# A Fourier mix with four mirrored tokens folded into each partition, and an order of work read from a table

## The chip, the cores and the metric

One core of a Trainium2 chip runs the whole program. The metric is device time in microseconds (us), from the first instruction to the last of one execution. TensorE (PE) does matrix products, VectorE (DVE), ScalarE (ACT) and GpSimd (POOL) work on elements, SyncE (SP) and POOL start DMAs. Each engine carries out its own instructions strictly in the order in which the program holds them, and waits on semaphores for the others.

## The reference

Three layers follow one another on 4 batches of 768 tokens, with 8 heads of 40 features (320 in all): a recurrence, a layer that mixes by Fourier transforms and a dense network, and a layer that mixes tokens by a network and then channels.

```python
for t in range(S):                                   # attention
    y[:, :, t] = einsum('bhd,bhde->bhe', rt, state)
    Sa = einsum('bhde,bhe->bhd', state, at)
    state = state * wt - outer(Sa, bt) + outer(vt, kt)

X = fft(fft(x, axis=1), axis=2)                      # moe: tokens (768), then features (320)
u = x + real(X)
un = (u - mean(u)) / sqrt(var(u) + 1e-6)
x = u + maximum(un @ w_ch1, 0) @ w_ch2               # 320 -> 1280 -> 320

h = maximum(xT @ w_tok1, 0) @ w_tok2                 # moe2: 768 -> 256 -> 768 over tokens
u = x + hT
out = u + maximum(u @ w_ch1, 0) @ w_ch2              # 320 -> 1536 -> 320
```

The input is real and only the real part of the transform is used: real(X)[t, f] = sum over tokens and features of x times cos(token angle + feature angle). So the sums of one token frequency t at feature frequency f are those of 768-t at 320-f.

## The kernel before

**Accuracy.** Products run in a reduced float32 form (fp32r) on two parts of each number: a high part that is rounded to 12 bits and the rest. One product is then three matmuls: high by high, high by low, low by high. Some matmuls are plain float32.

**Attention.** 768 tokens are cut in 12 chunks of 64. Per chunk there are decay scans on DVE, an inverse of a small matrix, and products on PE: `sc` (line 509), `y` (lines 527 and 531), `x`, `z`, `s`. The output y of chunks 0 to 8 goes through DRAM (`xd`) and is loaded into the token tiles `X`, [128 tokens, 6 tiles, 4 batches, 320]; that of 9 and 10 goes straight to X by DMA; that of the last is written by DVE (line 537).

**First transform, `fft(b)`, batch by batch.** Twice (even and odd frequencies): tiles k and k+3 are added or subtracted into F (line 845), features folded into `ef` (846 to 848), split into Xh on ACT (851, 854) and Xl on DVE (852, 855), and multiplied by the token table T1: pairs of a matmul by Xh with 384 or 388 columns (line 866) and one by Xl with half of them (line 867). There are 24 such pairs for a batch. ACT and DVE take the sums out of PSUM into five tiles A (873, 875, 877), and ACT copies each mirrored to columns 385 to 768 (881).

**Second transform, `fft2(b)`.** Six groups of 128 tokens, each 8 matmuls `mix` with 320 columns (line 896); DVE adds each to X (898) and takes the statistics of the norm (899, 900).

**Network.** `turn(b, half)` norms and turns 3 tiles of 128 tokens (`trp`, line 957, and `th`, `tl`); `ch` then runs per 128 hidden units a group `hps` of 8 matmuls (986), the positive part hh on ACT (988), the rest hl on DVE (989), and a group `acc` of 9 matmuls (976). There are 80 such groups on W1, W2 (the first dense network) and 96 on v1, v2.

**Weights.** They lie in DRAM as 64-bit floats and are taken apart on the chip: a `job` (line 807 on) loads 64-bit raw data (`mdraw`), has four DVE instructions (819, 820, 822, 823), one on ACT (821) and two on POOL (824, 825), and writes both parts to DRAM (m11h, m11l for W2), from where POOL's queue loads them (line 795). Two sets of buffers carry the jobs in turn.

**Order.** The program is written as operations with a cost, a due time, reads and writes. `Plan.emit` (line 100 on) puts them in order before the kernel is built: each engine takes the ready operation with the earliest due time, by modelled costs and a table of shifts. Where the model sees PE idle it puts fillers, `warm` matmuls (line 52) whose result nobody reads; each shows as two instructions in the trace.

The order on an engine that matters most is that behind the last y: what remains of fft(0), fft2(0), turn, fft(1), and the jobs for W2 all stand on DVE together.

Of the kernel before, what the change touches and what calls it, by code (L numbers as in the profile page):

```python
# [26 lines left out]
YB='y'

def layouts(r,k,v,w,a,b):
    def heads(x,fill=0.0):  # L30
# [23 lines left out]
DMAC={('dec2',0.61):(0.91, 0.31),('dec2',1.25):(1.56, 0.75),('inv',0.42):(0.05, 2.19),('inv',1.69):(1.13, 1.55),('kg',0.85):(1.63, 1.11),('kg',0.9):(1.03, 1.07),('load',0.05):(0.05, 1.78),('load',1.4):(1.4, 1.63),('load',2.82):(2.85, 2.04),('load2',1.46):(1.67, 1.54),('load3',1.3):(1.4, 1.7),('load3',1.92):(2.53, 1.39),('loada',0.71):(0.96, 1.53),('merge',0.45):(0.53, 1.47),('merge',0.9):(0.97, 1.13),('out_tile',1.2):(1.93, 0.12),('out_tile',2.4):(2.86, 0.57),('outp',0.46):(0.4, 1.24),('wdec',0.6):(0.62, 1.6),('wdec',1.2):(1.08, 1.88)}  # L54
LDMA=.81

class Op:
# [4 lines left out]
LATE_SAME={'DVE':.118,'ACT':.12,'POOL':.12}

class Plan:

    def __init__(s,banks):
        s.ops=[]; s.w={}; s.r={}; s.banks=banks; s.stage=None; s.filler=None
    def op(s,eng,cost,fn,R=(),W=(),due=None,alloc=None,free=(),data=0.0,rel=0.0,after=(),cols=0.0,pools=None,port=None,lag=.4,nd=8,cls=0,bulk=0):
        if eng=='SP' and s.stage: data,lag=DMAC.get((s.stage[0],round(data,2)),(data,lag))
        o=Op(); o.cols=cols; o.cls=cls; o.bulk=bulk; o.stage=s.stage; o.pools=pools; o.lag=lag; o.nd=nd; o.port=(eng=='POOL' and not data) if port is None else port; o.rel=rel; o.eng,o.cost,o.fn,o.due,o.data=eng,cost+EXTRA.get(eng,0.0),fn,due,data  # L70
        o.alloc=[] if alloc is None else alloc if isinstance(alloc,list) else [alloc]
        o.free=tuple(free); o.idx=len(s.ops); o.succ=[]
# [10 lines left out]
        for d in o.deps: s.ops[d].succ.append(o.idx)  # L83
        s.ops.append(o); return o
    def lat(s,a,b):
        if a.eng==b.eng: return .2 if a.eng=='SP' else LATE_SAME.get(a.eng,0.0)
        return LATE.get(a.eng,.2)
    def dur(s,o): return o.cost+ (1.8+o.data if o.eng=='SP' or o.data else 0)
    def grant(s,b):
        while s.seen<b:  # L90
            s.seen+=1; x=s.seen
            s.low[x]=sum(s.cols.get(y,0.0) for y in range(x-NBK,x))<HT
        return 1.0-.5*sum(s.low.get(y,True) for y in range(b-NBK+1,b+1))/NBK
    def pe(s,t,o):

        w=o.cost; c=o.cols/w; dt=TICK/NBK
        if o.cls!=s.cls: t+=SW; s.cls=o.cls
        while w>1e-9:
            k=int(t/dt); f=s.grant(k)
            d=min(w/f,(k+1)*dt-t+1e-6); w-=d*f; t+=d  # L100
            s.cols[k]=s.cols.get(k,0.0)+c*d*f
            s.hist.append((t-d,t,c*f))
        return t
    def emit(s,end,slack):
        s.cols={}; s.hist=[]; s.cls=0; s.low={}; s.seen=0
        ops=s.ops
        lst=[0.0]*len(ops)
        for o in reversed(ops):
            t=end if o.due is None else o.due
            for j in o.succ: t=min(t,lst[j]-(s.lat(o,ops[j])+s.dur(o))*slack)  # L110
            lst[o.idx]=t
        for o in ops:
            if o.stage: lst[o.idx]+=OFF.get(o.stage[0],0.0)+OFF.get(o.stage,0.0)
        engines={e:0.0 for e in ('PE','ACT','DVE','POOL','SP','NONE')}
        cand={e:[] for e in engines}
        def put(o):
            o.ready=max([o.rel]+[ops[d].fin+s.lat(ops[d],o) for d in o.deps]); cand[o.eng].append(o)
        for o in ops:
            o.nwait=len(o.deps); o.fin=None
        for o in ops:  # L120
            if o.nwait==0: put(o)
        dma=0.0; held=[None,0.0]; ring=[]; pushed=0
        def port(o): return held[1] if o.port and held[0]!=o.eng else 0.0
        free={b:[0.0]*n for b,n in s.banks.items()}; s.bank={}
        left={}
        for o in ops:
            for h in o.free: left[h]=left.get(h,0)+1
        n=0; pools=()
        def fill(t,end):

            w=sum(r*(min(b,end)-max(a,end-TICK)) for a,b,r in s.hist[-80:] if b>end-TICK)
            if w>=FILL[1]: return
            b=next(((b,j) for b in pools for j,x in enumerate(free[b]) if x<=t),None)
            m=0; top=-int(-(FILL[1]-w)//512); o=Op(); o.eng='PE'; o.idx=-1; o.cls=0; o.deps=[]; o.cost=FILL[0]; o.cols=512.0; a=t+.1
            while b and m<top and a+FILL[0]<=end: a=s.pe(a,o); m+=1
            if m==0: return
            o.cost=a-t; o.fin=a; o.nd=m; free[b[0]][b[1]]=a+.3; s.trace.append((t,o)); s.nfill+=m
            if not DRY: s.filler(*b,m)
# [1020 lines left out]
```

## Time and profile before

| | |
|---|---|
| median of 3 runs | 999.69 us |
| lowest, highest | 997.78, 1010.21 us |
| span of the profiled execution | 998.0 us |
| mean granted TensorE clock, share of full | 0.974 |
| PE busy | 940.2 us (94%) |
| DVE busy | 632.2 us (63%) |
| ACT busy | 439.2 us (44%) |
| POOL busy | 271.0 us (27%) |
| fft and fft2, PE: lines 866, 867, 896 | 29.9, 24.8, 31.0 us |

The span is that of one execution under the profiler; it is 1.7 us below the median of the timed runs. Busy times of neighbours on PE overlap, since one matmul begins while the one ahead is still draining, so the length of a row is more than what it adds; what it adds is read from one start to the next. A digit of the page's slices is the busy share of about 25 us in tenths.

### The profile page before, as it was taken

How to read it: one execution, taken by the hardware profiler on the slowest of the kernel's cores; microseconds unless marked ns; L12 is line 12 of the kernel's file. 1: busy time of each engine (PE TensorE's matmuls, PEld its weight loads, DVE VectorE, ACT ScalarE, POOL GpSimd, SP SyncE). 2: the span in 40 equal slices, each digit the busy share in tenths (PEclk: the TensorE clock that was granted, in tenths of full speed). 3: DMA queues.
4: the chain of work that ended last, by engine and by line, in shares of the span. 5: the costliest groups of instructions: out<-in, count | busy, mean ns of one | idle time of the engine just before them, and what ended most of it. 6: DMA issues, size and time to landing. Idle time of an engine off the chain costs nothing.

```text
span 998.0 us, 23467 instructions
## 1 busy us (share of the span) xinstructions
PE 940.2 (94%) x9571; PEld 893.7 (90%) x9571; DVE 632.2 (63%) x1401; ACT 439.2 (44%) x910; POOL 271.0 (27%) x372
## 2 busy tenths in 40 slices
PE   7548999999999998999999999999999999999998
PEld 6447788788788887899999999999999999999998
DVE  8799497878849348899799984324342632423332
ACT  5266879789697674333342322223221312112121
POOL 8123544344653524243343435000000000000000
PEclk9788999999899899899999999999999999999999
DMA  9986878999787788354454456800000201101110
GB/s 212 200 188 139 185 181 171 184 200 213 162 190 180 180 237 290 117 180 138 146 186 131 162 159 217 310 1 1 1 20 24 92 21 48 68 20 49 44 44 20
DMA packets 144750, 132.53 MB, mean 133 GB/s; under 512 B 101059, under 2 KB 121539, under 8 KB 144515
## 3 DMA queue, kind: packets, MB, share of 16 engines
q1 hardware_dynamic: 139843, 107.36, 42.7%
q0 software_dynamic: 4800, 23.67, 6.9%
q8 instruction: 75, 1.23, 0.5%
q14 instruction: 32, 0.26, 0.1%
HBM read 88.94 MB, written 37.29 MB: 126 GB/s over the span
## 4 chain that ended last, share of the span: by engine, by line
PE 52%; DVE 6%; DMA 1%; issue 1%; ACT 0%; SPq 0%; DVEq 0%; ACTq 0%
PE hps L986 22%; PE acc L976 21%; PE t2ps L1063 2%; PE tps L1050 2%; PE mix L896 2%; DMA mdraw<-in_moe_w_tok_dram 1%; PE psA L866 1%; PE trp L957 1%; DVE mda L820 1%; PE warm L52 1%; PE psA L867 0%; DVE F L845 0%; DVE hl L989 0%; DVE Xl L852 0%; DVE A L875 0%
## 5 line engine op out<-in xcount | busy, mean ns | idle before, releaser
L989 DVE SCALAR_TENSOR_TENSOR hl<-hps,hh 128x384 fp32r<-128x384 f32 x176 | 97.7, 556 | 225.3 <-ACT hh L988 224.5
L988 ACT ACTIVATE hh<-hps 128x384 fp32r<-128x384 f32 x176 | 86.2, 490 | 321.2 <-PE hps L986 320.9
L986 PE MATMUL hps<-th,v 128*128 128x384 f32 x576 | 142.4, 337 | 0.0
L976 PE MATMUL acc<-v,hh 128*128 128x320 f32 x576 | 128.0, 309 | 0.0
L986 PE MATMUL hps<-th,W 128*128 128x384 f32 x480 | 120.3, 339 | 1.2 <-DVE hl L989 0.8
L976 PE MATMUL acc<-W,hh 128*128 128x320 f32 x480 | 107.4, 310 | 0.5 <-DVE X L999 0.5
L986 PEld LDWEIGHTS hps<-th,v 128*128 128x128 f32 x576 | 103.7, 188 | 0.0
L976 PEld LDWEIGHTS acc<-v,hh 128*128 128x128 f32 x576 | 98.1, 188 | 0.0
L976 PE MATMUL acc<-v,hl 128*128 128x320 f32 x288 | 89.0, 309 | 0.0
L986 PEld LDWEIGHTS hps<-th,W 128*128 128x128 f32 x480 | 86.8, 187 | 2.3 <-DVE hl L989 1.5
L976 PEld LDWEIGHTS acc<-W,hh 128*128 128x128 f32 x480 | 81.2, 188 | 0.8 <-ACT hh L988 0.8
L824 POOL TENSOR_TENSOR mda<-mda,mdh 128x320 f32<-128x320 f32 (+2 forms) x44 | 44.7, 1016 | 122.3 <-ACT mdh L821 62.8
L329 POOL TENSOR_SCALAR_AFFINE_SELECT RT<-RT 64x384 f32<-64x384 f32 x72 | 53.5, 767 | 82.1 <-ACT RT L238 78.4
L976 PE MATMUL acc<-W,hl 128*128 128x320 f32 x240 | 74.0, 308 | 0.0
L319 PE MATMUL kg<-am,bt 120*128 120x192 f32 x242 | 51.3, 351 | 21.3 <-ACT am L238 18.1
L986 PE MATMUL hps<-tl,v 128*128 128x384 f32 x192 | 64.6, 337 | 0.0
L319 PEld LDWEIGHTS kg<-am,bt 120*128 120x128 f32 x242 | 40.3, 198 | 26.3 <-ACT am L238 18.9
L519 POOL TENSOR_SCALAR_AFFINE_SELECT sc<-sc 64x384 f32<-64x384 f32 (+1 forms) x72 | 41.5, 577 | 73.1 <-ACT sc L238 61.4
L509 PE MATMUL sc<-rm,VZd 120*128 120x192 f32 x264 | 57.7, 354 | 2.2 <-DMA VZd<-in_vR_dram 1.5
L52 PE MATMUL warm<-ident 128*128 128x128 f32 x346 | 52.0, 297 | 4.5 <-DVE A L877 2.5
L976 PEld LDWEIGHTS acc<-v,hl 128*128 128x128 f32 x288 | 54.1, 188 | 0.0
L986 PE MATMUL hps<-tl,W 128*128 128x384 f32 x160 | 53.9, 337 | 0.0
(176 smaller groups left out, 2025.0 us busy)
## 6 DMA issues: line engine op xcount, KB each, us to landing
bt<-in_bkR_dram SPq DMA_DIRECT2D x12, 660.0 KB
mdraw<-in_moe_w_ch_dram SPq DMA_DIRECT2D x22, 320.0 KB
wS<-in_wR_dram SPq DMA_DIRECT2D x12, 335.2 KB
a<-in_aR_dram SPq DMA_DIRECT2D x12, 335.2 KB
RT<-a SPq DMA_DIRECT2D x36, 111.7 KB
LT<-in_vT_dram SPq DMA_DIRECT2D x12, 330.0 KB
VZt<-in_vT_dram SPq DMA_DIRECT2D x12, 330.0 KB
VZd<-in_vR_dram SPq DMA_DIRECT2D x12, 330.0 KB
```

Of the source, the lines that this page charges most:

```text
L52: for x in range(m): nc.tensor.matmul(t[:,128*(x%4):128*(x%4)+128],lhsT=ident,rhs=ident,start=True,stop=True)
L319: nc.tensor.matmul(ps[:,192*x:192*x+192],lhsT=bt[:,g+x].rearrange("p v t -> p (v t)"),rhs=am[:,:,g+x],start=True,stop=True)
L329: nc.gpsimd.affine_select(out=kv,in_=kv,pattern=[[0,3*m],[1,L]],compare_op=ALU.is_gt,fill=0.0,base=0,channel_multiplier=-1)
L509: for x,g in enumerate(gs): nc.tensor.matmul(ps[:,192*x:192*x+192],lhsT=VZd[:,g].rearrange("p v t -> p (v t)"),rhs=s.rm[:,:,g],start=True, ...
L519: nc.gpsimd.affine_select(out=o,in_=o,pattern=[[0,3*m],[1,L]],compare_op=ALU.is_gt,fill=0.0,base=0,channel_multiplier=-1)
L824: P.op('POOL',.07+d*.00237,lambda: nc.gpsimd.tensor_tensor(out=g("da").bitcast(F32),in0=g("da").bitcast(F32),in1=g("dh").bitcast(F32),op=A ...
L896: nc.tensor.matmul(s.pst(h)[:,:320],lhsT=aa[:K,sl],rhs=T2[:K,tb],start=n==0,stop=n==7)
L976: nc.tensor.matmul(s.pst(acc[x]),lhsT=a[:,sl],rhs=t[w2][w][:,m],start=(m==0 and n==0),stop=(m==MT-1 and n==2))
L986: for n,(l,r) in enumerate(ops): nc.tensor.matmul(ps,lhsT=l,rhs=r,start=n==0,stop=n==7)
L988: s.act(384,lambda: nc.scalar.activation(out=t["hh"][z],in_=s.pst(h),func=AF.Relu),[kp],[('hh',z)],free=[h[0]])
L989: s.dve(.47,lambda: nc.vector.scalar_tensor_tensor(out=t["hl"][z],in0=s.pst(h),scalar=0.0,in1=t["hh"][z].bitcast(F32),op0=ALU.max,op1=ALU. ...
L1050: nc.tensor.matmul(s.pst(h),lhsT=t["k1"][x][:,k,ms],rhs=t[a][:,k],start=k==0 and n==0,stop=k==5 and n==2)
```

## The change

The tokens are laid out anew, so that partition p of tiles 0, 1 (and of 3, 4) holds tokens that are mirrors of one another: tile 0 holds p+1, tile 1 383-p, tile 3 767-p, tile 4 385+p; tiles 2 and 5 hold the 128 that remain twice over in halves. The attention writes y in that layout, for six chunks in reversed order of tokens, with a few more and shorter DMAs through `xd`; the host permutes the rows of w_tok1, w_tok2 and of the output to match.

The first transform adds and subtracts tile k and k+3 (FP, FM), folds features (ef), and then adds and subtracts tiles 0 and 1 (sd): a sum runs over 128 partitions and two parts where it ran over three. The table has 416 columns a frequency kind. Per batch there are 8 pairs (a matmul of 416 columns by Xh, one of 208 by Xl), one more matmul of 208 columns (Ds), and 9 plain float32 matmuls `psA` with 64 columns of weights and 208 moving columns (T1f), whose results go to the lower or the upper half of the partitions. Only 385 token frequencies are formed.

```diff
-                                nc.tensor.matmul(ps[:,:2*cn],lhsT=t["Xh"][:,k,o:o+128],rhs=T(k,tb,par,2*cn),start=n==1 and k0==0,stop=False)
-                                nc.tensor.matmul(ps[:,:cn],lhsT=t["Xl"][:,k,o:o+128],rhs=T(k,tb,par,cn),start=False,stop=n==w and k1==3)
...
+            for n,op in (("FP",ALU.add),("FM",ALU.subtract)):
+                s.dve(.06+.336*w,lambda n=n,op=op,K=K,k0=k0,k1=k1: V.tensor_tensor(out=t[n][:,K,:320],in0=x()[:,K],in1=x()[:,3+k0:3+k1],op=op),xk+['mid0',(n,'pad')],kk(n),port=True)
...
+                for z,op in enumerate((ALU.add,ALU.subtract)):
+                    s.dve(.44,lambda z=z,op=op: V.tensor_tensor(out=t["sd"][:,z],in0=t["ef"][:,0],in1=t["ef"][:,1],op=op),e2(0,1)+['mid'],[('sd',z)],port=True)
+            def split(z,src,rd):
+                s.act(353,lambda: nc.scalar.activation(out=t["Xh"][:,z],in_=src(),func=AF.Copy),rd+['mid'],[('Xh',z)])
+                s.dve(.44,lambda: V.tensor_tensor(out=t["Xl"][:,z],in0=src(),in1=t["Xh"][:,z].bitcast(F32),op=ALU.subtract),rd+[('Xh',z)],[('Xl',z)],port=True)
...
+            z=2 if part else (par if kind==0 else 1-par); tk=2*kind+par; o=pst(h)[r]
+            out=[(t["Xh"][:,z,cs],T(part,tk,TC),o[:,:TC]),(t["Xl"][:,z,cs],T(part,tk,HC),o[:,:HC])]
+            if part and kind==0 and par==1: out.append((t["Ds"][:,cs],at.T1[:,8*TC:8*TC+HC],o[:,:HC]))
...
+                            nc.tensor.matmul(pst(h)[64*par:64*par+64,:HC],lhsT=sd(part,par if kind==0 else 1-par)[:,TS[kind]],rhs=TF(part,2*kind+par),start=part==1 and kind==0,stop=part==0 and kind==1,skip_group_check=True)
+                    if part: nc.tensor.matmul(pst(h)[64:128,:HC],lhsT=t["dd"][:,TS[0]],rhs=at.T1f[:,4*TC:4*TC+HC],start=False,stop=False,skip_group_check=True)
```

The second transform has four groups of 8 matmuls with 322 columns. Each sum is added to X forward for one token and with its features reversed for the mirror token, so a batch has 7 adds on DVE (three forward of 128 rows, four mirrored of 128, 128, 96 and 32 rows) instead of 6. ACT's mirrored copies of A go.

```diff
-        for i in range(6):
-            xk=s.at.xb(i,b) if s.first[b] else []
+        for i,(r,cs) in enumerate(((slice(0,128),slice(0,128)),(slice(0,128),slice(256,384)),(slice(0,128),slice(128,256)),(slice(0,128),slice(288,416)))):
...
+            def mi(q,rows):
+                s.dve(.4,lambda h=h: V.tensor_tensor(out=x(q,rows),in0=s.pst(h)[rows,320:0:-1],in1=x(q,rows),op=ALU.add),[kp]+xk(q)+['pend'],[('x',q,b)],free=[h[0]])
```

The jobs of the weights have four sets of buffers instead of two (three for those of W2):

```diff
-        nc=s.nc; V=nc.vector; P=s.P; d=dh.shape[-1]; q=dl.shape[0]; j=0 if nm=="w2" and n<WE else n%2; due=rel+40
+        nc=s.nc; V=nc.vector; P=s.P; d=dh.shape[-1]; q=dl.shape[0]; j=n%3 if nm=="w2" else n%4; due=rel+40
```

The planner goes. A long string, `ORDER`, names every operation in the order in which it is emitted, its PSUM buffer, and the fillers (`+count,bank,buffer`):

```diff
-    def emit(s,end,slack):
+    def emit(s):
...
+        for x in ORDER.split():
+            if x[0]=='+':
+                m,b,j=x[1:].split(','); assert (b,int(j)) not in held
+                s.filler(b,int(j),int(m)); continue
+            x,_,js=x.partition(':'); o=ops[int(x,36)]
+            assert o.idx not in done and all(d in done for d in o.deps)
...
+            o.fn(); done.add(o.idx)
```

**PE, the end of the attention.** Before, from the last filler ahead of the last y on; `psA` with Xh and Xl are sums of fft(0), whose first 8 pairs already stand further up, between steps of the last chunk.

```order
L52 MATMUL warm<-ident 128x128 x2
L527 MATMUL y<-Sbd_151,r_139 64x120
L531 MATMUL y<-kbt_149,sc_154 64x40 x3
L52 MATMUL warm<-ident 128x128
L866 MATMUL psA_5211<-T_4831,Xh 128x388
L867 MATMUL psA_5211<-T_4831,Xl 128x194
L866 MATMUL psA_5211<-T_4831,Xh 128x388
L867 MATMUL psA_5211<-T_4831,Xl 128x194
L866 MATMUL psA_5227<-T_4831,Xh 128x388
L867 MATMUL psA_5227<-T_4831,Xl 128x194
L866 MATMUL psA_5235<-T_4831,Xh 128x388
L867 MATMUL psA_5235<-T_4831,Xl 128x194
```

The same place with the change:

```order
L54 MATMUL warm<-ident 128x128 x5
L425 MATMUL y<-Sbd_151,r_139 64x120 x2
L429 MATMUL y<-kbt_149,sc_153 64x40 x6
L425 MATMUL y<-Sbd_151,r_139 64x120
L429 MATMUL y<-kbt_149,sc_154 64x40 x3
L861 MATMUL psA_5385<-T1f,ef 64x208 x4
L862 MATMUL psA_5385<-T1f,dd 64x208
L846 MATMUL psA_5394<-T_4875,Xh 128x416
L846 MATMUL psA_5394<-T_4875,Xl 128x208
L846 MATMUL psA_5394<-T_4875,Xh 128x416
L846 MATMUL psA_5394<-T_4875,Xl 128x208
L861 MATMUL psA_5385<-T1f,sd 64x208 x4
```

No sum of fft(0) stands ahead of the last y any more; its float32 matmuls (T1f) come first.

**PE, ahead of fft2(0).** With the change, the rest of fft(0) and the fillers on both sides of it; `mix` is the first group of fft2(0):

```order
L54 MATMUL warm<-ident 128x128 x12
L846 MATMUL psA_5475<-T_4875,Xh 128x416
L846 MATMUL psA_5475<-T_4875,Xl 128x208
L846 MATMUL psA_5475<-T_4875,Ds 128x208
L846 MATMUL psA_5475<-T_4875,Xh 128x416
L846 MATMUL psA_5475<-T_4875,Xl 128x208
L846 MATMUL psA_5488<-T_4875,Xh 128x416
L846 MATMUL psA_5488<-T_4875,Xl 128x208
L846 MATMUL psA_5488<-T_4875,Xh 128x416
L846 MATMUL psA_5488<-T_4875,Xl 128x208
L54 MATMUL warm<-ident 128x128 x7
L894 MATMUL mix<-T_5364,A_5365 128x322 x2
```

Twelve and seven fillers stand here; before, 6 stand inside fft(0) and 11 ahead of the first mix. From the first sum of fft(0) behind the last y to the end there were 39 fillers, and are 76.

**POOL, the tables of W2.** `mda` are the two POOL steps of a job (m11l holds their results), `W<-m11h` and `W<-m11l` the loads of the first half of W2. Before:

```order
L824 TENSOR_TENSOR mda_4844<-mda_4844,mdh_4845 128x320
L825 TENSOR_TENSOR mda_4844<-mda_4844,mdt_4843 128x320
L824 TENSOR_TENSOR mda_5340<-mda_5340,mdh_5341 128x320
L825 TENSOR_TENSOR mda_5340<-mda_5340,mdt_5339 128x320
L824 TENSOR_TENSOR mda_4844<-mda_4844,mdh_4845 128x320
L825 TENSOR_TENSOR mda_4844<-mda_4844,mdt_4843 128x320
L795 DMA W_5482<-m11h 128x1600
L824 TENSOR_TENSOR mda_5340<-mda_5340,mdh_5341 128x320
L825 TENSOR_TENSOR mda_5340<-mda_5340,mdt_5339 128x320
L795 DMA W_5483<-m11l 128x1600
```

With the change:

```order
L805 TENSOR_TENSOR mda_5063<-mda_5063,mdt_5062 128x320
L805 TENSOR_TENSOR mda_5071<-mda_5071,mdt_5070 128x320
L804 TENSOR_TENSOR mda_5067<-mda_5067,mdh_5068 128x320
L775 DMA W_5451<-m11h 128x1600
L804 TENSOR_TENSOR mda_5071<-mda_5071,mdh_5072 128x320
L804 TENSOR_TENSOR mda_5063<-mda_5063,mdh_5064 128x320
L805 TENSOR_TENSOR mda_5067<-mda_5067,mdt_5066 128x320
L805 TENSOR_TENSOR mda_5063<-mda_5063,mdt_5062 128x320
L805 TENSOR_TENSOR mda_5071<-mda_5071,mdt_5070 128x320
L775 DMA W_5452<-m11l 128x1600
```

The steps of three jobs now alternate, and five of them stand between the load of the high part and that of the low part, where two stood.

## Rows read from the trace of the kernel before

**Rows 1.** The page, part 2: busy tenths in 40 slices

```profile
PE   7548999999999998999999999999999999999998
...
DVE  8799497878849348899799984324342632423332
```

**Rows 2.** The page, part 4: chain, shares by line

```profile
PE hps L986 22%; PE acc L976 21%; PE t2ps L1063 2%; PE tps L1050 2%; PE mix L896 2%; DMA mdraw<-in_moe_w_tok_dram 1%; PE psA L866 1%; PE trp L957 1%; DVE mda L820 1%; PE warm L52 1%; PE psA L867 0%; DVE F L845 0%; DVE hl L989 0%; DVE Xl L852 0%; DVE A L875 0%
```

**Rows 3.** Windows: PE, PEld, DVE, ACT, POOL busy (x), clock, DMA, GB/s

```profile
340.00:350.00 10.00, 10.00 (x167) 8.71 (x167) 1.44 (x4) 5.74 (x13) 5.32 (x15) 0.52 0.95 239
386.00:490.00 104.00, 96.31 (x610) 93.12 (x611) 94.14 (x252) 37.27 (x102) 36.67 (x43) 0.97 0.53 171
490.00:998.00 508.00, 504.60 (x3210) 502.95 (x3208) 246.80 (x573) 128.32 (x287) 60.53 (x70) 1.00 0.25 82
```

**Rows 4.** Timeline of PE (start, length): last y, fft, fft2

```profile
385.50 0.49 PE L531 MATMUL y<-kbt,sc 128*64 128x40 f32 x6
...
389.86 0.36 PE L866 MATMUL psA<-T,Xh 128*128 128x384 f32 x1
...
392.73 0.36 PE L866 MATMUL psA<-T,Xh 128*128 128x384 f32 x1
...
403.39 3.72 PE L896 MATMUL mix<-T,A 128*128 128x320 f32 x24
...
406.95 0.34 PE L866 MATMUL psA<-T,Xh 128*128 128x388 f32 x1
```

**Rows 5.** Timeline of PE: float32 matmuls of the attention, next rows

```profile
354.71 1.57 PE L509 MATMUL sc<-rm,VZd 120*128 120x192 f32 x8
356.11 0.37 PE L417 MATMUL pt<-ident,R 120*64 120x120 f32 x2
...
357.29 0.43 PE L527 MATMUL y<-Sbd,r 120*64 120x120 f32 x4
357.54 0.50 PE L531 MATMUL y<-kbt,sc 128*64 128x40 f32 x12
...
362.78 0.40 PE L527 MATMUL y<-Sbd,r 120*64 120x120 f32 x2
363.01 0.49 PE L531 MATMUL y<-kbt,sc 128*64 128x40 f32 x6
```

**Rows 6.** Lines of DVE, fft and fft2: xcount | busy us, mean ns

```profile
L852 DVE TENSOR_TENSOR Xl<-ef,Xh 128x384 fp32r<-128x384 f32 (+8 forms) x40 | 14.2, 379 | 1.6 <-ACT Xh L851 1.4
...
L898 DVE TENSOR_TENSOR X<-mix,X 128x320 f32<-128x320 f32 x24 | 11.5, 480 | 1.4 <-PE mix L896 1.2
...
L845 DVE TENSOR_TENSOR F<-X 128x960 f32<-128x960 f32 (+2 forms) x10 | 9.5, 948 | 1.0 <-DMA X<-xd 0.9
...
L875 DVE TENSOR_TENSOR A<-psA,A 128x193 fp32r<-128x193 f32 (+3 forms) x24 | 8.5, 357 | 0.9 <-ACT A L873 0.3
...
L877 DVE TENSOR_TENSOR A<-psA,A 128x193 fp32r<-128x193 f32 (+3 forms) x24 | 8.1, 353 | 0.4
...
L846 DVE TENSOR_TENSOR ef<-F 128x477 f32<-128x477 f32 (+2 forms) x10 | 5.5, 546 | 0.1
...
L855 DVE CAST Xl<-Xl 128x99 fp32r<-128x99 f32 (+5 forms) x20 | 5.4, 299 | 0.0
```

**Rows 7.** Timeline of PE: fillers, first hps, first acc

```profile
395.63 2.69 PE L52 MATMUL warm<-ident 128*128 128x128 f32 x22 [2.46 <-DVE A L877]
...
427.41 0.44 PE L986 MATMUL hps<-th,W 128*128 128x384 f32 x1 [0.38 <-DVE th L962]
...
437.06 0.45 PE L976 MATMUL acc<-W,hh 128*128 128x320 f32 x2
```

**Rows 8.** Timeline of DVE: the tenth hl

```profile
462.85 0.54 DVE L989 SCALAR_TENSOR_TENSOR hl<-hps,hh 128x384 fp32r<-128x384 f32 x1
```

**Rows 9.** Timeline of POOL: the load of W2's first low half

```profile
428.38 0.58 POOL L795 DMA_DIRECT2D W<-m11l  x1
```

**Rows 10.** DMA issues: KB each, median us to landing

```profile
W<-m11l POOLq DMA_DIRECT2D x2, 800.0 KB, 6.2
```

More of the change, by code (lines that the diff above doesn't have):

```diff
@@ L35, in layouts @@
     out={'rR':rows(r),'vR':rows(v)}
+    for i in RV: out['rR'][i]=out['rR'][i][...,::-1]
     out['wR']=np.concatenate([np.zeros((NSC,120,NG,1),w.dtype),rows(w,1.0)],3)
@@ L82, in op @@
         o.deps=sorted(deps)
-        for d in o.deps: s.ops[d].succ.append(o.idx)
         s.ops.append(o); return o
[L85 to L103, printed above, removed]
-    def emit(s,end,slack):
[L105 to L125, printed above, removed]
@@ L126, in emit @@
+    def emit(s):
+        ops=s.ops; done=set(); left={}; held={}
         for o in ops:
             for h in o.free: left[h]=left.get(h,0)+1
[L128 to L138, printed above, removed]
@@ L190, in emit @@
             for h in o.free:
                 left[h]-=1
[L192 to L197 removed]
+                if left[h]==0: del held[h[0],s.bank[h]]
+        assert len(done)==len(ops)
 class Attn:
@@ L879, in fft @@
-        for m in range(3):
-            for a in (2*m,2*m+1)[:2 if m<2 else 1]:
-                s.act(432,lambda a=a: nc.scalar.activation(out=t["A"][a][:,385:769],in_=t["A"][a][:,384:0:-1].bitcast(F32),func=AF.Copy),[('A',a)],[('Am',a)])
+        nc=s.nc; t=s.t; at=s.at; V=nc.vector
+        G=((1,3),(0,1)) if b==0 else ((0,3),)
+        if b==0: hs=[at.psum(x,[128,TC],f"psA{m}") for m,x in enumerate(PA)]; pst=at.pst
+        else: hs=[s.psum('ps',[128,TC],f"psA{m}") for m in range(5)]; pst=s.pst
@@ new lines, in emit, with main, f @@
+        def emit(l):
+            for a,m,o,st,sp in l: nc.tensor.matmul(o,lhsT=a,rhs=m,start=st,stop=sp,skip_group_check=True)
+        AK=lambda a: [('A',a)]
+        blocks=[(0,0),(0,1),(1,0),(1,1)]
+        MC=(slice(0,128),slice(225,353)); TS=(slice(128,192),slice(161,225))
+        def main(m,parts):
+            par,kind=blocks[m]; h=hs[m]
+            def f():
+                for part in parts: emit(mms(h,kind,par,part,MC[kind],slice(0,128),part==1,part==0))
+            s.pe(sum(.3+(.11 if part and kind==0 and par else 0) for part in parts),f,[y for part in parts for y in rk(part,par,kind)]+['mid'],[('psA',h[0])]+[('A',2*kind),('A',2*kind+1)],alloc=h[0] if 1 in parts else None,cols=624*len(parts))
@@ L883, in fft2 @@
+        if b==0:
+            for m in range(2): main(m,(1,))
+            tail((1,))
+            for m in range(2): main(m,(0,)); evac(m)
+            tail((0,)); evac(4)
+            for m in range(2,4): main(m,(1,0)); evac(m)
+        else:
+            for m in range(4): main(m,(1,0)); evac(m)
+            tail((1,0)); evac(4)
     def fft2(s,b):
         nc=s.nc; t=s.t; V=nc.vector
-        x=lambda i: s.at.X[:,i,b]
-        for i in range(6):
-            xk=s.at.xb(i,b) if s.first[b] else []
+        x=lambda i,r=slice(0,128): s.at.X[r,i,b]
@@ L1157 @@
     r = _run(nc, [feed], core_ids=[0])
-    return r.results[0]["out_0_dram"]
+    out = np.empty((4, 768, 320), np.float32)
+    out[:, tk] = r.results[0]["out_0_dram"]
+    return out
```

454 lines of the change are left out of this document (239 added, 215 removed), and 4 rows, old and new, of the table OFF.

## The prediction

> **What bounds the kernel now.** I read the page's slices first. They show where in the span an engine is full [rows 1]: PE's digit is 9 in nearly every slice from the sixth on, while DVE's is 8 or 9 only as far as about the 26th and then falls to 2 to 4. So there are two regimes. The chain of waits says the same by line [rows 2]: hps and acc, the dense networks on PE, carry 43% of the span; the lines of this change on PE, mix and psA, 2% and 1%; DVE's lines 1% or less each. That would make the change worth little, but a chain follows only the path that ended last, and every matmul that stands in PE's queue ahead of it counts too. So I go by windows [rows 3]. Behind 490 us PE is busy 504.6 of 508 us at full clock: what is taken from PE there is saved, provided that DVE (246.8 of 508) follows. From 386, where the last y ends [rows 4], to 490, PE is busy 96.3 of 104 us at a mean granted clock of 0.97, and DVE 94.1. In that stretch DVE carries fft, fft2, the norm and the jobs of the weights at once, and PE is partly filled with fillers. The timeline shows it: PE stands idle 2.46 us for DVE's evacuation of A, then runs 22 filler instructions, then mix [rows 7]; and the first hps at 427.41 waits for DVE's th. What the change is worth is decided by how much DVE has to do there, not by PE alone.
>
> **PE, the first transform.** Eleven pairs start from 389.86 to 392.73, so ten steps take 2.87 us [rows 4]: 0.287 for 384+192 columns, and 24 of them 6.9 us a batch. A new pair has 416+208 columns; scaled by columns it costs 0.311, eight of them 2.49, and the single matmul of 208 columns 0.10. The float32 matmuls have no row of their own shape. From both sides: `sc`, float32 with 192 columns, appears as two instructions a matmul, and four matmuls take from 354.71 to 356.11 [rows 5], 0.35 each, so 0.38 for 208 columns. If nine run one behind the other that is 3.4 us a batch. In `y` the two float32 matmuls of a pair write to two halves of the partitions, as the new ones do: a pair takes 0.25 us, the one at the end that has no partner 0.23 [rows 5]. So a partner costs a tenth more, four pairs cost 4 x 0.41 and the last 0.38: 2.0 us. I take 2.0, since y has the very form of these matmuls, and keep 3.4 as the end. Together 4.6 for 6.9: 2.3 us less.
>
> **PE, the second transform.** 24 mix take from 403.39 to 406.95 [rows 4], 0.148 each. 48 were 7.1 us; 32 of 322 columns are 4.8: 2.3 us less. Per batch 4.6 to 4.7, over four batches **18.6 us less work on PE** (13.1 if the halves don't overlap). Below that there is no bound from rows: nothing else of PE's is removed.
>
> Where the trace has a matmul with its weight load behind another on the same 128 rows, the load leaves hardly a gap: a mix takes 0.148 us for 320 columns [rows 4], where a column a cycle at the full clock of 2.4 GHz would be 0.133, an estimate. The Trainium skill (TensorE: Matmul & The Clock Gate, Part 3: Packing small matmuls) says that a weight load overlaps matmuls in flight only when their row groups differ. By that rule the tails, all on the same 128 rows, would run one behind the other and the saving would be the 13.1; the mix rows speak against it.
>
> **DVE.** Per batch before, from the lines over four batches [rows 6]: F 9.5, ef 5.5 and about as much again for the second line, Xl 14.2 and 5.4, evacuation 8.5 and 8.1; 56.7 in all, 14.2 a batch. After: FP and FM 2 x 1.14, two ef 1.1, two sd and three Xl at about 0.53, two small ones 0.5, ten evacuations 3.6: 10 us. The seventh add of X costs 0.48 [rows 6]; a reversed operand stands in ef's row too and isn't dearer there. So 3.7 us less a batch. ACT loses its mirrored copies and more; I cost that at nothing, since DVE paces the stretch and ACT is busy a third of it [rows 3]. The twelve short DMAs on SP in the attention and the reversed reads I cost at nothing as well: they are hidden behind a chunk of the recurrence, about 30 us; their price if a chunk waited is one landing, some 6 us [rows 10].
>
> **What the order does with it.** In the attention the rows on PE are the same up to about its eighth chunk. At its end, eight pairs of fft(0) no longer stand ahead of the last y, so that ends 8 x 0.287 = 2.3 us earlier, near 383.7. Behind it, I priced every row of PE and DVE in the two orders by the rows above, up to the tenth hl, which in the trace ends at 463.4 [rows 8].
>
> - Before: PE's own work to there is 53.8 us (104 psA, 96 mix, 18 trp, 80 hps, 63 acc). It had 77.4 us, so 23.6 went to fillers, waits and half clock. DVE had 64.8 priced us for 76.4 of time, 1.18 of time per priced us.
> - After: PE's own work is 49.3 (78 psA, 72 mix, the rest the same). DVE has 72.2, more than before, although the transforms are cheaper: 61 instructions of the jobs instead of 44, four more adds of X and their statistics, and the transform of batch 2 are drawn ahead of this hl. The fillers agree with it: 72 instead of 36 stand ahead of the tenth hps group, 0.245 us each [rows 7].
>
> At 1.18, DVE would come there 85.2 us after the last write of X (near 384.7), at 469.9. PE's spare time would be 469.9 - 383.7 - 49.3 = 36.9, that is 13.3 more than before. At 1.00, with DVE never waiting, it would be about as before. DVE's busy share of the stretch is 0.905, and the rest are waits, many of them for raw data of the jobs, which now have more buffers. I take the middle, 1.12: 465.6, a spare of 32.6, **9.0 us given back**. Where a stall of PE for A goes, the hl are late next.
>
> **The sum.** 998.0 - 18.6 + 9.0 = 988.4 against the profiled span; the median of the runs shown is 1.7 above the span and their fastest 0.2 below it. I forecast **988**. This case's own range is 983 to 994, from the two ends of DVE's pace and half of the tails' bound.
>
> **Rivals.**
>
> *All of it arrives.* DVE does not set the pace after all, since the work it has drawn ahead is missing later and PE has groups to run meanwhile (buffers for three hh and hl). Then 998.0 - 18.6 = 979.4. For it: the sums behind 490 are saved in any case, and DVE's load per batch is 3.7 lower. Against: the fillers. If the new order also escapes the half clock of 340 to 350 (granted 0.52, 4.8 us lost there [rows 3]), it is 975; the attention's order is nearly the same there, which speaks against that. Chance 0.28 for below 983, of which 0.20 lie under 979.7.
>
> *The halves run one behind the other.* 5.5 us more PE work; where PE waits for DVE anyway (batches 0 and 1) it costs nothing, so about 3 us: 991, inside the forecast's range. Chance 0.15, counted with the forecast.
>
> *Everything is given back.* DVE's pace stays at 1.18 or worse and the tails are dear: 998.0 - 13.1 + 13.3 = 998. Chance 0.15 for 994 to 999.7.
>
> *Slower: the low half of W2 comes late.* The first acc, at 437.06 [rows 7], needs W2's low half, whose load POOL starts at 428.38 [rows 9] and which lands 6.2 us later [rows 10], at 434.6. In the new order five steps of three alternating jobs stand on POOL between the two loads, where two stood, and those need DVE and ACT. If that puts the landing off, the first acc waits and PE behind it. PE's own work up to there is 31.3 before and 28.8 after, so at an unchanged 437 already 437 - 383.7 - 28.8 = 24.5 us are spare where 19.7 were, 4.8 given back; each us later is lost whole. From 437 + 13.8 = 451 on the kernel is slower than before; at 455 it takes 1002. Against it: 23 instructions of the jobs stand on DVE ahead of the first hl, where 21 stood, so the jobs are no further behind. Chance 0.08. A loss of over 2% would need the acc at 471: 0.03.
>
> That the fold doesn't remove the work it claims is no rival of weight: the rows on PE are counted in the order.
>
> **Numbers.** 988, with 0.49 for the forecast's own case; the rivals have 0.28, 0.15 and 0.08. The range of 976 to 1000 leaves out about 0.06 below and 0.08 above. Two per cent of 999.69 is 20 us, about what a measurement of this kernel tells from no change (its runs lie 12 us apart): faster is under 979.7, slower over 1019.7. Faster 0.20, within 2% 0.77, slower 0.03.
>
> **What the profile after would show.** Right: pairs of 0.31 us, the tail near 2.0 us a batch (3.4 if it is serial), mix 0.149; the last y near 384; from 490 on PE full; up to the tenth hl fillers and waits of PE of 28 to 37 us, with DVE at 9 or more tenths and the hl or th as the releasers. Wrong: the tenth hl ahead of 460, or PE without fillers' worth of waits there (then it is the first rival), the first acc behind 445 with a DMA or POOL's W as its releaser (the last), or a stretch of half clock where there was none.

## The result: 1.0% faster, nearly all of it gained ahead of the last y

| | before | after |
|---|---|---|
| median of 20 runs each, on the same chips | 1003.0 us | 992.64 us |
| lowest, highest | 996.48, 1012.38 | 984.53, 1001.65 |
| ratio of the times, with its 95% interval | | 0.9897 [0.9868, 0.9926] |
| profiled execution: its time, its span | span 998.0 | 996.21, span 994.5 |

The forecast of 988 had the ratio at 0.988. So the number held, but by luck: two of its terms were off in opposite directions and nearly cancelled, as the profile of the changed kernel shows. Its page, part 2, tenths of PE, DVE and of the granted clock [rows 1]:

```profile
PE   7558989999899998888999999999999999999998
...
DVE  8799489896958637999898873324333442333422
...
PEclk9687999999999998999999999999999999999999
```

The two regimes stand as before: DVE at 8 or 9 into the 23rd slice, PE full behind it. (In the kernel before, DVE's digits fall behind the 24th slice [rows 1]; the prediction read the 26th.) To compare, I cut both executions at the last y and at the end of the tenth hl. Windows of the kernel before (columns as in [rows 3]):

```profile
386.00:463.40 77.40, 70.73 (x451) 68.14 (x452) 73.77 (x210) 29.71 (x85) 26.52 (x32) 0.96 0.56 185
463.40:998.00 534.60, 530.19 (x3369) 527.93 (x3368) 267.17 (x615) 135.88 (x304) 70.68 (x80) 1.00 0.26 84
```

The same two stretches with the change:

```profile
383.50:471.00 87.50, 76.14 (x510) 69.24 (x506) 83.44 (x218) 26.68 (x66) 31.61 (x39) 0.98 0.58 192
471.00:994.50 523.50, 518.26 (x3280) 513.74 (x3280) 247.47 (x576) 124.38 (x275) 67.95 (x76) 1.00 0.25 83
```

The first stretch is 10.1 us longer, the second 11.1 shorter. Behind the last y both kernels take the same: 998.0 - 385.5 = 612.5 and 994.5 - 383.2 = 611.3 us. The work taken from PE there is given back. DVE looks like the engine that sets the first stretch: it is busy for 83.4 of 87.5 us, and its waits there come to 2.6 us (engine, line, waited for: total, times, longest):

```profile
DVE X L898 <- PE mix L894: 2.3, 1, 2.3
DVE y L910 <- ACT y L909: 0.3, 1, 0.3
```

The tenth hl on DVE, the first of these two, ends at 471.0 [rows 8]:

```profile
470.52 1.01 DVE L994 SCALAR_TENSOR_TENSOR hl<-hps,hh 128x384 fp32r<-128x384 f32 x2
```

PE's timeline shows the single steps [rows 4, 5, 7]:

```profile
383.21 0.23 PE L429 MATMUL y<-kbt,sc 128*64 128x40 f32 x1
...
393.75 3.16 PE L54 MATMUL warm<-ident 128*128 128x128 f32 x14 [2.64 <-DVE A L873]
...
403.19 0.37 PE L846 MATMUL psA<-T,Xh 128*128 128x416 f32 x1
...
403.49 0.37 PE L846 MATMUL psA<-T,Xh 128*128 128x416 f32 x1
...
404.18 0.92 PE L861 MATMUL psA<-T1f,ef 128*64 128x208 f32 x8
404.93 0.34 PE L861 MATMUL psA<-T1f,sd 128*64 128x208 f32 x1
...
406.09 1.16 PE L54 MATMUL warm<-ident 128*128 128x128 f32 x8
...
417.95 0.44 PE L991 MATMUL hps<-th,W 128*128 128x384 f32 x1
...
434.99 0.54 PE L981 MATMUL acc<-W,hh 128*128 128x320 f32 x2
```

A pair takes 0.30 us, the nine float32 matmuls of batch 1 from 404.18 to 406.09, 1.91. PE still stands idle for DVE's A (2.64 us). The first hps is 9.5 us earlier than before, the first acc 2.1, no more than the last y itself. On POOL the two loads of W2's first half have moved apart, to 8.5 us from 7.0, but the second starts earlier than before [rows 9]:

```profile
417.98 0.58 POOL L775 DMA_DIRECT2D W<-m11h  x1
...
426.49 0.58 POOL L775 DMA_DIRECT2D W<-m11l  x1
```

Ahead of the last y, the first `zt` of the tenth chunk and the last y mark the end of the attention. Before, profiled a second time under the label before_again:

```profile
320.50 0.68 PE L502 MATMUL zt<-ident,VZt 64*120 64x64 f32 x8
384.43 0.49 PE L531 MATMUL y<-kbt,sc 128*64 128x40 f32 x6
```

and after:

```profile
327.41 0.69 PE L400 MATMUL zt<-ident,VZt 64*120 64x64 f32 x8
```

From that mark to the last y it is 62.9 (322.6 to 385.5 in the first profile) and 63.9 us before, 55.8 after. The profiled execution after came to the mark 5 to 7 us later and made that up, so the two spans hide most of this gain.

### The profile page after: what moved, and what is told of

It reads as the page before. It is cut to its first block, busy times and chain, and to the rows that moved or that the text cites. A ratio compares the mean times of both kernels' runs of the same rounds, so it can differ in the third digit from the quotient of the medians.

```text
span 994.5 us, 23178 instructions
## 1 busy us (share of the span) xinstructions
PE 931.1 (94%) x9525; PEld 882.5 (89%) x9525; DVE 617.9 (62%) x1345; ACT 422.4 (42%) x846; POOL 269.8 (27%) x368
## 4 chain that ended last, share of the span: by engine, by line
PE 64%; DVE 15%; DMA 6%; ACT 3%; issue 2%; SPq 1%; POOL 1%; DVEq 0%; ACTq 0%; POOLq 0%
PE hps L991 23%; PE acc L981 22%; PE sc L407 3%; PE t2ps L1068 2%; PE tps L1055 2%; PE kg L216 2%; DVE pr L250 2%; SPq L134 1%; PE y L429 1%; PE s L368 1%; PE y L425 1%; DMA VZt<-in_vT_dram 1%; DVE Mt L251 1%; DMA X<-xd 1%; PE mc L302 1%
## 5 line engine op out<-in xcount | busy, mean ns | idle before, releaser
L991 PE MATMUL hps<-th,v 128*128 128x384 f32 x576 | 144.4, 339 | 0.0
L991 PEld LDWEIGHTS hps<-th,W 128*128 128x128 f32 x480 | 86.9, 188 | 6.1 <-DVE hl L994 2.7
L226 POOL TENSOR_SCALAR_AFFINE_SELECT RT<-RT 64x384 f32<-64x384 f32 x72 | 52.4, 750 | 85.9 <-ACT RT L136 81.9
L54 PE MATMUL warm<-ident 128*128 128x128 f32 x416 | 62.4, 301 | 4.7 <-DVE A L873 2.6
L407 PE MATMUL sc<-rm,VZd 120*128 120x192 f32 x264 | 60.2, 364 | 4.0 <-DMA VZd<-in_vR_dram 2.1
L54 PEld LDWEIGHTS warm<-ident 128*128 128x128 f32 x416 | 57.7, 213 | 5.9 <-issue 3.2
```

Of the source, the lines that this page charges most:

```text
L54: for x in range(m): nc.tensor.matmul(t[:,128*(x%4):128*(x%4)+128],lhsT=ident,rhs=ident,start=True,stop=True)
L226: nc.gpsimd.affine_select(out=kv,in_=kv,pattern=[[0,3*m],[1,L]],compare_op=ALU.is_gt,fill=0.0,base=0,channel_multiplier=-1)
L407: for x,g in enumerate(gs): nc.tensor.matmul(ps[:,192*x:192*x+192],lhsT=VZd[:,g].rearrange("p v t -> p (v t)"),rhs=s.rm[:,:,g],start=True, ...
L991: for n,(l,r) in enumerate(ops): nc.tensor.matmul(ps,lhsT=l,rhs=r,start=n==0,stop=n==7)
```

## The experiments

Each run is cut at the same marks. Times in us; "hl" is the end of the tenth hl behind the start of the last y, "profile only" a kernel that was run once. The last y is read where its row begins; in before, before_again, before_pairs, both_late, oldplan and tail_order that row holds three matmuls, and begins 0.3 us ahead of the last. All runs but oldplan and the three of before order the attention as the changed kernel does; they differ from it behind the last y alone.

| run | zt to y | y to hl | y to end | span | ratio to before |
|---|---|---|---|---|---|
| before | 62.9 | 77.9 | 612.5 | 998.0 | |
| before_again | 63.9 | 77.2 | 611.3 | 995.7 | |
| after | 55.8 | 87.8 | 611.3 | 994.5 | 0.9897 [0.9868, 0.9926] |
| more_early | 56.0 | 88.2 | 611.6 | 986.5 | 0.9855 [0.9766, 0.9944] |
| more_late | 58.8 | 88.8 | 619.4 | 998.0 | 0.9875 [0.9829, 0.9921] |
| nofill | 59.7 | 87.9 | 611.4 | 1008.2 | profile only |
| oldplan | 63.7 | 86.9 | 614.7 | 1020.1 | 1.0129 [1.0036, 1.0223] |
| before_pairs | 66.5 | 83.7 | 619.3 | 1020.9 | 1.0067 [1.0025, 1.0108] |
| both_late | 54.8 | 79.2 | 636.2 | 1023.7 | 1.0116 [1.0070, 1.0162] |
| paced_both | 60.6 | 79.1 | 618.6 | 1011.3 | 0.9978 [0.9932, 1.0025] |
| paced_f3 | 55.6 | 82.0 | 609.5 | 985.5 | profile only |
| paced_fast | 53.5 | 80.9 | 631.0 | 1013.9 | 1.0064 [1.0013, 1.0114] |
| paced_fast_nf | 56.0 | 80.1 | 632.7 | 1020.1 | profile only |
| tail_order | 54.9 | 86.6 | 610.1 | 998.9 | profile only |

**Does DVE set the pace behind the last y? more_early and more_late** add 38 fillers each, once in twelve places ahead of the tenth hps, once in one place near 500 us. The lines shown are entries of `ORDER`.

```diff
-+12,y,0
++18,y,0
...
-+7,acc,0
++11,acc,0
```

> The changed kernel with 38 more fillers (9.3 us of PE at 0.245 each), spread over the places between the last y and the tenth hps group where fillers stand already (72 become 110). My theory: up to the tenth hl DVE sets the pace and PE has 38 us of fillers and waits there, so the fillers go into waits: the stretch from the last y to the end stays within 3 us of the changed kernel's 611, and the waits of PE in it shrink. Rival (PE's work counts everywhere): 8 to 9 us longer.

```diff
-+1,ps,0
++39,ps,0
```

> The changed kernel with the same 38 fillers at one place behind the tenth hl, near 500 us. My theory: behind that point PE is the bound, so all 9.3 us show: the stretch from the last y to the end is 8 to 10 us longer than in the changed kernel. Rival (DVE still sets the pace there): under 4 us.

Windows of more_early from the last y to the tenth hl:

```profile
374.90:463.10 88.20, 81.96 (x591) 76.54 (x589) 84.44 (x219) 27.00 (x67) 31.30 (x39) 1.00 0.59 191
```

and of more_late from there to the end:

```profile
467.40:998.00 530.60, 526.34 (x3356) 522.22 (x3356) 247.76 (x576) 124.23 (x275) 67.88 (x76) 1.00 0.25 82
```

Both came as expected. Ahead of the tenth hl the fillers vanish in PE's spare time: PE is 5.8 us busier than after, its waits shrink from 10.3 to 5.4 us, and the end comes 611.6 behind the last y. Near 500 us they cost 8.1. So PE's work doesn't set the first stretch, and does set the second. The timed medians lean the same way (992.5 and 998.2 us), but the ratios can't show it: their intervals are wider than 8 us, since the executions differ by more than that ahead of the last y.

**nofill** takes all fillers behind the last y away.

```diff
-+12,y,0
-+7,acc,0
...
-+3,acc,0
```

> The changed kernel without any filler behind the last y (76 fewer, 18.6 us of PE). If the fillers only lie in waits and do nothing else, the stretch from the last y to the end stays at 611 within 2 us, with 18 us more of waits in PE. My theory: they also hold the clock; without them the granted clock of the stretch up to the first acc falls from about 0.97 to 0.7 to 0.9, and the stretch is 3 to 10 us longer.

Its windows, two of the slices of 10 us:

```profile
420.00:430.00 10.00, 6.90 (x26) 5.36 (x25) 8.65 (x30) 2.69 (x7) 2.20 (x3) 0.54 0.32 106
...
440.00:450.00 10.00, 4.78 (x21) 3.82 (x22) 9.86 (x25) 2.00 (x5) 2.26 (x4) 0.73 0.44 133
```

The granted clock falls as expected, to 0.54 and 0.73 of 2.4 GHz in these slices, so for a good part of them to the lower level; PE is busy 6.9 and 4.8 of the 10 us, DVE 8.7 and 9.9. Yet the end stays 611.4 behind the last y, where I expected 3 to 10 us more. A lower clock cost nothing where DVE is the one waited for; the fillers neither helped nor harmed there.

**Fold or order? oldplan and before_pairs.** The first takes the change's arithmetic and orders it by the planner of before (with its costs and due times); the second takes before's own order, written out, and moves the 8 pairs of fft(0) behind the last y.

```diff
-            at.P.emit()
+            at.P.emit(TM + 560, SLACK)
```

> The changed arithmetic, layout and buffers, but the order made by the old planner with its old shifts, in place of the fixed table. Theory (the fold takes 18.6 us from PE, and DVE's queue gives back about half whichever order stands): 0.5 to 1.5% faster than before, as the changed kernel. Rival (the gain is the new order's): no faster than before, or slower, since the old shifts were made for other operations.

```diff
+        if (MOVE and n<last and pe(o) and o.stage==('fft',0)) or not ready(o):
+            q.append(o)
```

> The kernel before, its order written down as it is and altered in one thing: the eight pairs of fft(0) that stand between steps of the last chunk go behind the last y. In three profiles with the changed kernel's order the time from the tenth chunk's zt to the last y is 55 to 58 us, in two of the kernel before 63 to 65. My prediction's account (the pairs take 8 x 0.287 us there): 2 to 3 us shorter, 60 to 62, and the stretch behind the last y at most 2.3 us longer than 612. Rival (the pairs sit on the recurrence's chain and cost more than their own length): 56 to 58, and the kernel 4 to 6 us faster than before.

Under the old planner the fold is slower than before by 1.3%, against my theory, and the end of the attention is as long as before's, 63.7 us. So the shorter end comes with the new order, not with the fold. Behind the last y, too, the fold alone brings nothing there: 614.7 us. But the planner's shifts were made for other operations, and its last y came at 405.4, so the run doesn't price the fold under an order made for it.

That the 8 pairs alone explain the shorter end isn't borne out: without them before's end takes 66.5, where I expected 60 to 62 or, by the rival, 56 to 58. The execution has slices of lower clock (0.72 to 0.77), but the timed runs are 0.7% slower as well. Where the pairs stood, PE now waits for ACT:

```profile
384.62 0.50 PE L441 MATMUL pt<-ident,R 120*64 120x120 f32 x3 [1.79 <-ACT PT L262]
```

So part of their time had filled a wait. The run speaks against the pairs as the whole cause; which of the other moved rows does it isn't settled.

**before_again** is the kernel before, unchanged, under the profiler.

> The kernel before, profiled once more. In the first profile its last y ends at 386.0 and 612.0 us follow. Since the attention's order is nearly the same in both kernels, I expect its end to move from execution to execution by several us (375 to 390, as in three kernels with the changed order of one attention) and the 612.0 to stay within 1 us. Rival: the attention ends near 386 each time, and what moves is behind it.

Its 63.9 and 611.3 us lie within 1.2 of the first profile, so the marks repeat, and the 7 us at the attention's end are not one execution's chance. The last y moved by 1.1 us only, where I expected several.

**Can DVE's work be put where DVE has room? both_late** moves 25 instructions of the jobs and the 11 of batch 3's transform from ahead of the tenth hl to behind the twelfth. Rows of DVE's order:

```diff
-TENSOR_TENSOR FP<-X 128x3x320
-TENSOR_SCALAR mdt2<-mdraw2 128x256
-TENSOR_SCALAR mdt1<-mdraw1 128x256
 SCALAR_TENSOR_TENSOR hl0<-hps,hh0 128x384
...
 SCALAR_TENSOR_TENSOR hl0<-hps,hh0 128x384
+TENSOR_SCALAR mdt3<-mdraw3 128x256
+TENSOR_TENSOR FP<-X 128x3x320
```

> The changed kernel with only the order of two kinds of work altered: what stands of the jobs of the second layer's weights (25 instructions on DVE) and of the first transform of batch 3 (11 on DVE) ahead of the tenth hl is moved behind the twelfth, with what depends on it, and has caught up by the 24th. My theory (DVE's load ahead of the tenth hl gives back the saving): about 13 us of DVE work less there, the tenth hl 10 to 16 us earlier than the 471 of the changed kernel, and the end 4 to 9 us earlier, since DVE has to catch up by the 24th. Rival (DVE's load is not what holds PE): no change within 2 us, or slower because raw data come late.

The tenth hl comes 8.6 us earlier (I expected 10 to 16), and the end 24.9 later, where I expected it 4 to 9 us earlier. Waits of PE from 500 to 600 us in it:

```profile
PE acc L972 <- DVE hl L985: 6.4, 1, 6.4
PE hps L982 <- DVE X L889: 4.9, 2, 3.9
PE trp L953 <- DVE hl L985: 4.1, 1, 4.1
PE mix L885 <- DVE hl L985: 3.1, 1, 3.1
```

The moved work stands in DVE's queue ahead of what PE needs next, so the spare time that DVE has there on average [rows 3] is not there at that moment. And the time that it freed on DVE went unused. Windows of 80 us from 40 us behind the last y on, in both_late and in the changed kernel:

```profile
427.50:507.50 80.00, 71.22 (x461) 68.59 (x459) 55.62 (x132) 21.26 (x50) 17.38 (x22) 0.98 0.32 102
423.20:503.20 80.00, 72.63 (x470) 68.96 (x470) 75.29 (x169) 25.43 (x60) 32.65 (x36) 1.00 0.54 175
```

DVE is busy 55.6 us where it had been 75.3, while PE gets through no more. The rival's late raw data are there too, but small: DVE waits 3.6 us for them in two places.

**paced_both, paced_f3** spread it: at most 2.4 instructions of the jobs behind each hl, and from the ninth hl 1.2 of the transform; paced_f3 moves the transform alone:

```diff
-TENSOR_TENSOR FP<-X 128x3x320
...
 SCALAR_TENSOR_TENSOR hl2<-hps,hh2 128x384
+TENSOR_TENSOR FP<-X 128x3x320
...
 SCALAR_TENSOR_TENSOR hl0<-hps,hh0 128x384
+TENSOR_TENSOR FM<-X 128x3x320
```

> The changed kernel, order alone altered: the jobs of the second layer's weights go on DVE only right behind an hl, at most 2.4 instructions each, and the 11 early DVE instructions of batch 3's transform right behind the ninth hl on, 1.2 each; 16 and 1 of them stand ahead of the tenth hl, where 25 and 11 stood. Nothing has to catch up at once. My theory (DVE's queue ahead of the hl holds PE): the tenth hl comes 8 to 11 us earlier than 87.5 behind the last y, and the stretch from the last y to the end is 3 to 8 us shorter than the changed kernel's 611.0. Rival (both_late was slow because DVE's load does not matter and raw data were late): 611 or longer.

> As paced_both, but only batch 3's 11 instructions are moved; the jobs stay. My theory: the tenth hl 5 to 7 us earlier than 87.5 behind the last y, the stretch to the end 2 to 5 us shorter than 611.0. Rival: no change.

Windows of paced_f3:

```profile
376.00:458.00 82.00, 73.90 (x514) 68.10 (x512) 77.14 (x209) 25.32 (x63) 30.57 (x38) 1.00 0.62 203
458.00:985.50 527.50, 519.30 (x3282) 513.68 (x3280) 254.56 (x586) 126.05 (x279) 70.30 (x77) 1.00 0.25 82
```

The tenth hl is 5.8 us earlier, as expected, but the second stretch grows by 4.0 though PE is busy only 1.0 us longer in it: the waits move. The end is 1.8 us nearer, just short of the 2 to 5 expected, in a single execution, and two profiles of the kernel before differ by 1.2. With the jobs moved too (paced_both) the tenth hl comes 8.7 us earlier, as expected, and the end 7.3 us further, not nearer. That profile caught the longest of ten executions; the timed ratio, 0.9978 against 0.9897 after, says the same.

**paced_fast** carries the jobs at 1.6 instructions per hl up to the eleventh and 3.1 from there, to be done sooner; **paced_fast_nf** is the same without the 30 fillers behind the first hps (the expectation counts four more).

```diff
-TENSOR_SCALAR mdt2<-mda2 128x256
 SCALAR_TENSOR_TENSOR hl2<-hps,hh2 128x384
+TENSOR_SCALAR mdt2<-mda2 128x256
```

> As paced_both, but the jobs take at most 1.6 instructions of DVE behind each of the first eleven hl and 3.1 from then on, so that they end as early as in the changed kernel (all by the fiftieth hl; paced_both ended later, and PE waited 4 us for DVE between 610 and 642). 13 and 1 instructions stand ahead of the tenth hl instead of 25 and 11. My theory: the tenth hl 8 to 10 us earlier than 87.8 behind the start of the last y matmul, as in paced_both (79.1), and the stretch to the end 2 to 6 us shorter than the changed kernel's 611.3. Rival (DVE as a whole is full up to about the twentieth hl, whatever stands first): 609 to 613, the waits only move behind the tenth hl.

```diff
-+1,acc,0
-+10,acc,0
...
-+3,acc,0
```

> As paced_fast, and without the 30 fillers behind the first hps and the 4 in the rest (8.3 us of PE). If PE now gets its hl in time, the fillers are in the way: 2 to 6 us shorter than paced_fast. If DVE still sets the pace, the same within 1 us, as without fillers in the changed kernel.

Waits of PE in paced_fast, 470 to 640 us:

```profile
PE hps L982 <- DVE X L887: 5.2, 2, 4.3
PE trp L953 <- DVE tl L957: 3.3, 1, 3.3
PE hps L982 <- DVE hl L985: 2.9, 1, 2.9
```

Neither account held: the tenth hl comes 6.9 us earlier, but the end is 631.0 behind the last y, 19.7 worse than after, and PE waits for DVE at hps and trp alike. Without the fillers it is 1.7 us longer still, so they were not in the way. No order that I tried clearly beats the changed kernel's, and none shows that a better one doesn't exist.

**Why does the tail cost 1.9 us? tail_order** exchanges two loops, so that float32 matmuls that follow one another write to the same half of the partitions.

```diff
-                    for kind in range(2):
-                        for par in range(2):
+                    for par in range(2):
+                        for kind in range(2):
```

> The changed kernel with the loops of the float32 tail exchanged: two matmuls to the lower half of the partitions, then two to the upper, where they alternated. If halves overlap because neighbours write to different ones, four matmuls take 0.38 + 0.38 + 0.41 = about 1.15 us instead of about 0.8, so the nine take 2.5 to 2.9 us a batch instead of 1.9. Rival (they overlap in any order, or not at all): 1.9 either way. The end moves by less than 2 us.

```profile
408.65 0.93 PE L861 MATMUL psA<-T1f,ef 128*64 128x208 f32 x8
409.41 0.34 PE L861 MATMUL psA<-T1f,sd 128*64 128x208 f32 x1
...
410.57 1.16 PE L54 MATMUL warm<-ident 128*128 128x128 f32 x8
```

From 408.65 to 410.57 it is 1.92 us, as before the exchange; four ef matmuls take 0.76, 0.19 each. So the rival holds: the two halves don't have to alternate for that.

## Why the prediction was right in its number and wrong in its parts

| term | predicted | profiled after |
|---|---|---|
| last y ends | 383.7 (-2.3) | 383.4 |
| from there to the tenth hl | 81.9 (+4.5) | 87.5 (+10.1) |
| from there to the end | 522.8 (-11.8) | 523.5 (-11.1) |
| span | 988.4 | 994.5 |

**The failed step: "I take the middle, 1.12".** From the last write of X, which ends at 385.3, DVE's time per priced us was (471.0 - 385.3) / 72.2 = 1.19; the upper end that I had from before, 1.18, was right. (The middle of 1.00 and 1.18 would have been 1.09; nothing in the rows gave 1.12.) I had argued that a tenth of the stretch was waits, many of them for raw data. That was read over 386 to 490. Waits of DVE in the kernel before over just that stretch:

```profile
DVE mdt L819 <- DMA mdraw<-in_moe_w_tok_dram: 5.1, 3, 2.8
DVE X L898 <- PE mix L896: 1.2, 3, 0.6
DVE hl L989 <- ACT hh L988: 0.9, 2, 0.6
```

All of the 5.1 us for raw data lie behind 463.4; from 386 to 463.4 the waits come to 2.5 us. So most of 1.18 was not waiting: 73.8 busy us stood against 64.8 priced, my prices being short by 14%, and the 2.5 us and short gaps between instructions made the rest. Part of the shortfall lies in single instructions: in this stretch 11 of them (13 with the change) took 0.15 to 1.0 us longer than the median of their line and shape, 5.9 us together (6.5); what held them isn't shown. The price should have been 1.18. By my own working that gives 469.9 and 13.3 us given back instead of 9.0, and a sum of 992.7. PE's spare came to 87.5 - 49.3 = 38.2 us, above the 28 to 37 that I gave. more_early and nofill show that PE's work and clock don't set this stretch, and five runs with less work on DVE ahead of the tenth hl reached it 5.8 to 8.7 us sooner. That the end would follow the tenth hl, none of them shows: DVE is busy 36.4 of the 40 us from 503.2 on in the changed kernel, so its pace reaches past that hl.

**DVE's saving per batch** was about 3 us, not 3.7. Lines of DVE after [rows 6]:

```profile
L872 DVE TENSOR_TENSOR A<-psA,A 128x208 fp32r<-128x208 f32 (+1 forms) x24 | 8.8, 369 | 0.8 <-ACT A L871 0.4
L898 DVE TENSOR_TENSOR X<-mix,X 128x320 f32<-128x320 f32 (+2 forms) x16 | 7.8, 487 | 4.1 <-PE mix L894 3.9
L896 DVE TENSOR_TENSOR X<-mix,X 128x320 f32<-128x320 f32 x12 | 5.8, 479 | 0.1
...
L836 DVE TENSOR_TENSOR Ds<-dd,Ds 32x161 fp32r<-32x161 f32 x4 | 1.9, 464 | 0.1
L834 DVE TENSOR_TENSOR dd<-FM 32x161 f32<-32x161 f32 x4 | 1.8, 462 | 0.2
```

All lines of the transforms come to 44.3 us, 11.1 a batch where I had 10. With the 14.2 that I had for before, that and the dearer adds leave 2.6; but I had left out the copies of L848, 1.6 us over four batches, which go, so it is 3.0. The two small ones (L834, L836), which I took for 0.5 together, are 0.93. The adds to X rose from 11.5 to 13.6, 0.5 a batch as predicted; on 128x320 the reversed ones (L898) took 482 ns, the others 479.

**PE's work was right.** Pairs of 0.30 (0.311 predicted), the tail 1.91 (2.0), a mix 0.149 to 0.157 (8 in 1.19 us from 419.45, 24 in 3.77 from 396.67; 0.149). The second stretch shrank by 11.1 for 11.8. The tail's reason was wrong, though: I took `y` to show that two halves of the partitions overlap, and tail_order finds the same price without the alternation. What rows show is that these float32 matmuls, with 64 columns of weights, cost half of what I scaled from `sc` with 128; that the columns are the reason isn't tested. By the rule of the Trainium skill (TensorE: Matmul & The Clock Gate, Part 3: Packing small matmuls) tails on the same 128 rows would not overlap their loads and would have cost more; neither run bears that out.

**The attention's end was mis-sized.** I gave it 2.3 us for the eight pairs. From the first zt of the tenth chunk to the last y, before has 63.4 in the mean of two executions, the new order 56.6 in the mean of ten (53.5 to 60.6): 6.8. Most of it arises between the first zt of the eleventh chunk and that of the twelfth: 22.2 and 26.6 us before, 18.1 after (17.4 to 22.4 in the ten). The eight pairs stand there and take 3.0 us in the first profile (367.54 to 370.57) and 3.9 in the second (366.30 to 370.17; the granted clock is 0.69 over 365 to 370.5), not 2.3; the second also stands idle for 2.5 us there. The first profile's stretch of 0.52 of the clock [rows 3] lies ahead of that, between the tenth chunk's zt and the eleventh's. With 0.6 behind the last y that makes 7.4 of the 10.4 us between the medians. The other 3 I can't place: the start up to the tenth chunk differs by 18 us from execution to execution (319 to 337) under one and the same order, and both profiles of before (998.0 and 995.7) are among its shorter executions.

**Why the number held all the same.** The sum had 2.3 us gained ahead of the last y and 7.3 behind it; measured are 6.8 and 0.6. Two errors of 4.5 and 6.7 us nearly cancelled. That is luck: the working foresaw neither. Of the 6.7 us the failed step is 4.3.

**The rivals.** "All of it arrives" fell: PE's saving didn't reach the end. "Everything is given back" was right about the stretch behind the last y, and wrong about the end, since the attention gave what it did not count. "Slower", by W2's low half, fell: its load starts 1.9 us earlier than before, and the first acc runs at 435.0. "The halves run one behind the other" fell with the tail's 1.91.

## What to carry to other kernels

Where one engine paces a stretch, price that stretch by the time that it took per unit of its work, and before calling any of it waiting, read that engine's waits over exactly that stretch. Here work saved on another engine ahead of such a point was worth nothing, and work of the pacing engine pushed behind it came back as waits, since it stands in order ahead of what is needed next, while the time that it freed went idle. Where executions differ more than the change does, cut them at an instruction that both have, and compare the parts.

## What the runs showed that was not expected

- A float32 matmul with 64 columns of weights and 208 moving columns costs 0.19 us, in either order of the halves; `sc`, with 128 and 192, costs 0.35 [rows 5].
- A granted clock of 0.54 to 0.73 in slices that DVE paces cost nothing: 611.4 us from the last y to the end without fillers, 611.3 with them.
- An add on DVE over 32 partitions and 161 elements took 0.32 us in three of four executions and 0.87 to 0.89 in the fourth (L834, L836; their mean is 0.46). Over 128 partitions it took 0.31 for as many elements, so fewer partitions saved nothing. Single instructions that take some 0.5 us longer than their like stand all over DVE's stretch:

```profile
380.46 0.31 DVE L823 TENSOR_TENSOR ef<-FP 128x161 f32<-128x161 f32 x1
...
402.19 0.89 DVE L836 TENSOR_TENSOR Ds<-dd,Ds 32x161 fp32r<-32x161 f32 x1
...
446.70 0.32 DVE L836 TENSOR_TENSOR Ds<-dd,Ds 32x161 fp32r<-32x161 f32 x1
```

- One and the same order of the attention reached its last y between 375 and 397 us in ten executions.
